# A gated linear attention feeding a silu layer on one core: silu tiles kept in matmul order, stores in two transfers, and a new order of the instructions

## The chip, the cores and the metric

The kernel runs on one core of one Trainium2 chip. The core has a matrix engine (TensorE, PE in the profile; its weight loads are PEld), a vector engine (VectorE, DVE), a scalar engine for table functions (ScalarE, ACT), GpSimd (POOL) and SyncE (SP), which here only issues transfers. All of them share sixteen DMA engines. The metric is the device time of one execution in microseconds: 178.47 us median of three runs before the change (178.16 to 179.44).

## The reference

For each of 4 batches and 8 heads, a 48 x 48 state is decayed row by row and updated at each of 768 steps, and read with q. The results of all heads form rows of 384 numbers, which go through a layer of 2048 units with silu:

```python
f = 1.0 / (1.0 + np.exp(-f_logit))
for t in range(S):                                   # 768 steps
    state = f[:, :, t, :, None] * state + np.einsum('bhd,bhe->bhde', k[:, :, t], v[:, :, t])
    y[:, :, t] = np.einsum('bhd,bhde->bhe', q[:, :, t], state)
x = y.transpose(0, 2, 1, 3).reshape(3072, 384)       # tokens by (head, dim)
h = x @ w_in                                         # 384 -> 2048
out = (h / (1.0 + np.exp(-h))) @ w_out               # 2048 -> 384
```

Inputs and the output are float32; the matmuls take bfloat16.

## The kernel before, in words

The 768 steps are cut into three windows of 256 tokens. A window of one batch is a block, numbered 4 x window + batch, so there are twelve blocks (0 to 11), and block D + 4 needs the state that block D leaves. A partition holds two neighbouring tokens (r = 0 and 1), so a block of 256 tokens fills 128 partitions, and inside a block there are two chunks of 64 partitions (f = 0 and 1).

The program is a list of tokens, the string PLAN, and `emit` turns each token into its instructions. The order of the tokens is the order in which each engine gets its instructions; nothing is reordered later. A token is a kind, a block and mostly a half of the heads, and `@v`, `@p`, `@a` or `@s` names the engine where there is a choice (VectorE, GpSimd, ScalarE, SyncE). Every tile lives in one of a fixed number of buffers per class (the table SLOTS), handed out in the order of the list, so the order also sets which transfer or matmul waits for which buffer. There are 8 PSUM banks, 21 wide buffers for loads and 4 output buffers.

The kinds that the text speaks of:

- ldf, ldq, ldk, ldv (L278): loads of a block's gate, q, k and v, of 384 KB each, or halves of 192 KB for blocks 0 and 1. WI and WO (L413, L415) load the layer's weights, CI and CO cast them to bfloat16.
- E, L, F1, IA, A, AX (L280 to L298): exponentials and logarithms of the gates on ScalarE; SA and CS sum them (CS on PE, L288 and L291). They and silu need different function tables, so ScalarE loads a table at each turn (L426).
- K1, KI, Q1, QG (L302 to L313): q and k times their decays.
- TQ with QC, or TD (L326): the transpose of q and k, on PE for the first blocks and by a DMA transpose for blocks 4 to 11. SC (L335) are the score matmuls, two PSUM banks a token; AT (L341) masks them; Y, YS (L349, L356) form the outputs.
- DP, SD, SU (L374 to L381): the state's increment, sum and decay.
- YC, then YT with XC or YD (L368): the output's copy out of PSUM and its transpose, into the tile xT.
- MI (L390): six matmuls, xT by 256 columns of w_in: one hidden group. SI (L394): silu of that group into the tile hT. MO (L400): four matmuls of hT by w_out: one output group; four of them make 128 tokens' outputs. OC copies them out of PSUM, SO (L408) stores a block.
- W (L422): matmuls on an idle tile, which fill PE's time where it would otherwise wait.

The outputs' partitions have two tokens' places interleaved until silu: the token at (f, r, c) is row 128 f + 2 c + r of its block. Before the change silu itself puts the tokens in their order while it writes hT, so that an output tile's partitions are consecutive rows. One line does that, with steps of two elements on the written side:

```python
nc.scalar.activation(T[1][:, 2 * j:2 * j + 2].rearrange("p n (f c r) -> p (n f) r c", f=2, r=2),
                     T[0].rearrange("p (m r c) -> p m r c", m=4, r=2), AF.Silu)
```

The last block's second half of tokens (f = 1) is computed in two column ranges (LAST: 0 to 256, 256 to 384) that are copied and stored apart, and its first half by itself.

Of the kernel before, what the change touches and what calls it, by code (L numbers as in the profile page):

```python
# [24 lines left out]
    ldf.1.1@s E.1.1 L.1.1 SA.1.1@v W.19:CS.1.1 CS.1.1 W.2:CS.0.0 ldf.0.0@s E.0.0 L.0.0 SA.0.0@v CS.0.0 W.4:CS.0.1  # L25
    ldf.0.1@s ldq.1.1@s ldk.1.1@s ldq.0.0@s ldf.1.0@s E.0.1 IA.1.1 L.0.1 F1.0.0 A.1.1 AX.0.0 F1.1.1 F1.0.1 IA.0.0
    Q1.1.1@v K1.1.1@v SA.0.1@p CS.0.1 W.8:TQ.1.1 A.0.0 IA.0.1 A.0.1 E.1.0 KI.1.1@p QG.1.1@v ldq.0.1@s ldk.0.1@s L.1.0
    TQ.1.1 W.8:CS.1.0 QC.1.1@a K1.0.1@p ldk.0.0@s ldq.1.0@s ldk.1.0@s ldv.0.1@s ldf.2@s ldv.0.0@s ldv.1.1@s ldv.1.0@s
    Q1.0.0@v SA.1.0@p CS.1.0 IA.1.0 F1.1.0 AX.1.0 A.1.0 QG.0.0@v Q1.0.1@v QG.0.1@v KI.0.1@v K1.0.0@p KI.0.0@p SC.1.1
    TQ.0.1 W.3:TQ.0.0 AX.0.1 QC.0.1@a K1.1.0@p KI.1.0@p AM.0@p Q1.1.0@v TQ.0.0 W.2:SC.0.1 AT.1.1 QG.1.0@v ldf.3@s  # L30
    WI.0@s WI.5@s WI.4@s ldq.2@s WI.2@s ldk.2@s WI.1@s WI.3@s WI.7@s WI.6@s ldv.2@s WO.0@s WO.1@s SC.0.1 W.5:TQ.1.0
    AT.0.1 TQ.1.0 QC.0.0@a E.2.0 AX.1.1 L.2.0 SC.0.0 W.3:DP.0 AT.0.0 VB.0@p SA.2.0@p DP.0 VB.1@p QC.1.0@a E.2.1
    CS.2.0 L.2.1 AX.2.0 SA.2.1@p AM.1@p SU.0.0@v SC.1.0 Y.0.0 Y.0.1 YC.0.0@a F1.2.0 IA.2.0 E.3.1 DP.1 AT.1.0 YS.0.1
    W.3:Y.1.0 CI.0@p SU.1.0@v YC.0.1@v Y.1.0 Y.1.1 YS.1.1 F1.2.1 E.3.0 YC.1.1@a CI.5@p YC.1.0@v YT.0.0 YT.0.1 CS.2.1
    XC.0.1@a XC.0.0@v YT.1.1 YT.1.0 AX.2.1 L.3.0 L.3.1 SA.3.1@p CI.2@p MI.0.0 XC.1.1@v XC.1.0@v CI.7@p F1.3.0 CI.4@a
    A.2.0 MI.1.0 IA.2.1 A.2.1 VB.2@p AM.2@p SD.1.1 SD.0.1 Q1.2.0@v Q1.2.1@v SA.3.0@v QG.2.1@v QG.2.0@v K1.2.0@v
    KI.2.0@v WO.2@s ldf.4@s WO.3@s ldq.3@s ldk.3@s WO.4@s WO.7@s WO.5@s ldk.4@s WO.6@s ldq.4@s MI.1.5 MI.1.4 MI.0.4
    MI.0.5 SI.1.4 MI.0.2 SI.0.5 SI.1.5 CS.3.0 CS.3.1 MI.1.2 SI.0.2 SI.1.0 SI.0.0 TQ.2.0 CI.1@v MI.1.1 MI.0.1 SI.1.2
    SI.0.4 SI.1.1 SI.0.1 K1.2.1@v KI.2.1@v CI.3@v TQ.2.1 QC.2.0@v QC.2.1@v CO.0@p CO.1@p MI.0.3 SI.0.3 SC.2.0 SC.2.1
    AT.2.0 AT.2.1 CI.6@a MI.0.7 MI.1.7 MI.1.6 MI.1.3 SI.1.7 SI.0.7 SI.1.6 SI.1.3 DP.2 Y.2.0 Y.2.1 ldf.6@s ldv.4@s  # L40
    ldv.3@s MI.0.6 SU.2.0@v YS.2.1 SI.0.6 E.4.0 IA.3.0 F1.3.1 L.4.0 IA.3.1 E.4.1 A.3.0 L.4.1 AX.3.0 F1.4.0 AX.3.1
    A.3.1 F1.4.1 CO.2@p K1.3.0@p SA.4.0@p KI.3.0@p SU.0.1@p K1.3.1@p SA.4.1@p KI.3.1@p K1.4.1@p CO.6@p K1.4.0@p
    YC.2.0@v YT.2.0 XC.2.0@v YC.2.1@v SD.2.1 MO.1.1.0 MO.0.1.0 YT.2.1 XC.2.1@v CO.3@v MO.0.0.0 MO.1.0.0 MI.2.7 MI.2.3
    MO.1.0.1 MO.0.0.1 MO.0.1.1 MO.1.1.1 Q1.3.0@v Q1.3.1@v QG.3.0@v QG.3.1@v MI.2.2 SI.2.7 SI.2.2 MI.2.1 SI.2.1 SI.2.3
    MI.2.0 MI.2.6 SI.2.6 SI.2.0 MI.2.4 MI.2.5 SI.2.4 CO.4@v CO.7@v SU.2.1@v CO.5@v TQ.3.0 MO.2.1.0 MO.0.0.2 SI.2.5
    QC.3.0@a MO.1.1.2 CS.4.1 MO.2.1.1 CS.4.0 MO.0.1.2 IA.4.1 MO.0.1.3 TQ.3.1 AX.4.1 IA.4.0 MO.2.1.2 MO.2.1.3 A.4.1
# [55 lines left out]
LAST = ((0, 256), (256, 384))  # L102

SET_OF = {x: "natural_log_exp_and_others" for x in ("E", "L", "F1", "IA", "A", "AX")} | {"SI": "silu_and_others"}


def uses(t):

# [18 lines left out]
    if kind == "CS":  # L127
        return [I("s", D), I("ps", "cs", D, a[1])]
# [359 lines left out]
```

## Time and profile before

| what | value |
|---|---|
| median of 3 runs | 178.47 us (178.16 to 179.44) |
| the profiled execution's own time | 179.7 us |
| its span in the profile | 178.0 us |
| PE busy | 169.2 us, 95% |
| PE's weight loads | 127.6 us, 72% |
| ACT busy | 134.8 us, 76% |
| DVE busy | 102.3 us, 57% |
| POOL busy | 62.2 us, 35% |
| DMA | 36.02 MB, mean 202 GB/s |
| granted clock of PE | full in all slices |

A row of a group reads: line, engine, operation, tile written <- tile read, shape, count; then busy time in us, mean ns of one; then the engine's idle time just before them and what ended it. A row of a timeline has its start and length in us, then engine, line, operation and count, and in brackets the idle time before it with what ended it. A matmul's end is modelled, so a busy PE is not necessarily PE at its peak, and back-to-back instructions overlap, so a group's busy time is less than count times mean.

### The profile page before, as it was taken

The page shows a single profiled execution, that of the slowest core. Times are in us where ns is not written, and L with a number is a line of the kernel's source. Part 1 is how long each engine was busy: PE and PEld are TensorE (multiplying, and loading weights), DVE is VectorE, ACT ScalarE, POOL GpSimd, SP SyncE. Part 2 cuts the span into 40 slices and gives each one's busy share as a digit, 9 for nine tenths or more (in the row PEclk, how much of TensorE's full clock was granted, in tenths as well). Part 3 has the DMA queues.
Part 4 walks back from the last instruction along what each step waited for, and adds up shares of the span by engine and source line. Part 5 has one row for each costly group of instructions (what it writes and reads, how often), then busy time and mean ns, then how long its engine had stood idle before and what let it go on. Part 6 is the DMA issues. An engine that isn't in the chain of part 4 may idle for free.

```text
span 178.0 us, 5593 instructions
## 1 busy us (share of the span) xinstructions
PE 169.2 (95%) x2281; PEld 127.6 (72%) x2281; DVE 102.3 (57%) x247; ACT 134.8 (76%) x289; POOL 62.2 (35%) x106
## 2 busy tenths in 40 slices
PE   7789999999999999999999999999979999999992
PEld 5567787867767787767688767688747688866661
DVE  6499887569148992497755586597784520000021
ACT  4989999799999899779899976899624029892410
POOL 6389512639562595104642230464003000000010
PEclk9999999999999999999999999999999999999999
DMA  5999999999929999999999998786993526000033
GB/s 136 296 299 323 311 344 363 333 292 341 258 40 215 299 130 230 201 267 269 155 206 247 213 297 225 174 209 120 315 208 103 90 48 251 18 0 0 0 131 137
DMA packets 81850, 36.02 MB, mean 202 GB/s; under 512 B 73824, under 2 KB 81664, under 8 KB 81824
## 3 DMA queue, kind: packets, MB, share of 16 engines
q1 hardware_dynamic: 81184, 34.35, 77.5%
q0 software_dynamic: 224, 0.79, 1.1%
q10 hardware_dynamic: 416, 0.52, 0.8%
q8 instruction: 18, 0.29, 0.7%
q14 instruction: 8, 0.07, 0.1%
HBM read 25.17 MB, written 4.72 MB: 168 GB/s over the span
## 4 chain that ended last, share of the span: by engine, by line
PE 46%; issue 20%; ACT 12%; DMA 10%; SPq 8%; DVE 1%; POOL 1%; DVEq 0%; ACTq 0%; POOLq 0%
PE ps L400 23%; PE ps L390 14%; ACT hT L394 11%; SPq L278 7%; DMA wide<-in_moe_w_in_dram 4%; DMA qkT<-qk 3%; DMA out_dram<-o 3%; PE ps L335 2%; PE ps L349 2%; SPq L413 2%; PE ps L356 2%; PE ps L288 1%; PE ps L374 1%; DVE sd L379 1%; PE ps L322 1%
## 5 line engine op out<-in xcount | busy, mean ns | idle before, releaser
L394 ACT ACTIVATE hT<-ps 128x512 bf16<-128x512 f32 x96 | 60.2, 788 | 13.7 <-PE ps L390 13.5
L400 PE MATMUL ps<-w_out_sb,hT 128*128 128x384 bf16 (+2 forms) x400 | 67.9, 320 | 0.2 <-ACT hT L394 0.2
L390 PE MATMUL ps<-xT,w_in_sb 128*128 128x256 bf16 x576 | 66.4, 273 | 0.4 <-DMA xT<-yb 0.3
L390 PEld LDWEIGHTS <-w_in_sb 128*128 128x128 bf16 x576 | 55.5, 98 | 9.1 <-DMA xT<-yb 0.6
L400 PEld LDWEIGHTS <-hT 128*128 128x128 bf16 x400 | 36.7, 98 | 21.0 <-ACT hT L394 0.2
L341 DVE TENSOR_TENSOR atm<-ps,mask 128x512 bf16<-128x512 f32 x48 | 30.3, 682 | 5.8 <-PE ps L335 5.5
L274 DVE COPY o<-ps 128x384 f32<-128x384 f32 (+2 forms) x9 | 4.6, 508 | 31.5 <-issue 28.2
L313 DVE TENSOR_TENSOR qk<-wide,ps 128x192 bf16<-128x192 f32 x48 | 14.4, 346 | 7.9 <-ACT ps L296 5.6
L308 POOL TENSOR_TENSOR qk<-wide,ia 128x192 bf16<-128x192 f32 x24 | 15.0, 647 | 5.3 <-ACT ar L298 2.9
L274 ACT COPY o<-ps 128x384 f32<-128x384 f32 x16 | 7.6, 482 | 11.4 <-PE ps L400 10.0
L286 POOL TENSOR_TENSOR s<-lf 128x192 bf16<-128x192 bf16 x15 | 8.5, 570 | 21.5 <-ACT lf L282 16.9
L381 POOL TENSOR_TENSOR st<-sd,al 128x384 bf16<-128x384 f32 x12 | 10.2, 855 | 15.1 <-DVE sd L379 7.6
L302 POOL TENSOR_TENSOR wide<-wide,f 128x192 f32<-128x192 f32 x17 | 11.0, 654 | 10.1 <-DMA wide<-in_k_dram 9.7
L379 DVE TENSOR_TENSOR sd<-ps,st 128x384 f32<-128x384 f32 x16 | 8.6, 550 | 9.1 <-PE ps L374 7.0
L280 ACT ACTIVATE e<-wide 128x384 f32<-128x384 f32 x24 | 12.0, 519 | 1.6 <-DMA wide<-in_f_logit_dram 1.4
L408 POOL DMA_DIRECT2D out_dram<-o x2 | 1.6, 816 | 32.4 <-ACT o L274 32.4
L282 ACT ACTIVATE lf<-e 128x384 bf16<-128x384 f32 x24 | 11.9, 520 | 0.3
L308 DVE TENSOR_TENSOR qk<-wide,ia 128x192 bf16<-128x192 f32 x24 | 10.5, 482 | 2.1 <-POOL wide L302 2.0
L426 ACT ACT_TABLE_LOAD x9 | 11.5, 1283 | 0.2
L274 POOL CAST vb<-wide 128x768 bf16<-128x768 f32 x7 | 5.8, 832 | 14.8 <-DMA wide<-in_v_dram 14.4
L422 PE MATMUL ps<-idle 128*128 128x256 bf16 x57 | 9.8, 320 | 1.3 <-DVE idle L434 1.3
L304 DVE SCALAR_TENSOR_TENSOR wide<-e,wide 128x192 f32<-128x192 f32 x24 | 9.9, 434 | 1.6 <-DMA wide<-in_q_dram 1.6
(60 smaller groups left out, 170.2 us busy)
## 6 DMA issues: line engine op xcount, KB each, us to landing
wide<-in_f_logit_dram SPq DMA_DIRECT2D x10, 384.0 KB, 5.5
wide<-in_q_dram SPq DMA_DIRECT2D x10, 384.0 KB, 6.2
wide<-in_k_dram SPq DMA_DIRECT2D x10, 384.0 KB, 5.8
wide<-in_v_dram SPq DMA_DIRECT2D x10, 384.0 KB, 5.5
wide<-in_moe_w_in_dram SPq DMA_DIRECT2D x8, 384.0 KB, 6.2
wide<-in_moe_w_out_dram SPq DMA_DIRECT2D x8, 384.0 KB, 6.3
out_dram<-o SPq DMA_DIRECT2D x8, 384.0 KB, 3.9
wide<-in_f_logit_dram SPq DMA_DIRECT2D x4, 192.0 KB, 3.2
```

The source lines that it names most:

```text
L274: copy = lambda o, i: E.copy(o, i) if eng == "a" else E.tensor_copy(o, i)
L278: E.dma_start(out=T[0][:, hs], in_=SRC[kind[2]][w, b][:, hs])
L280: nc.scalar.activation(T[1][:, hs], T[0][:, hs], AF.Exp, scale=-1.0)
L282: nc.scalar.activation(T[1][:, hs], T[0][:, hs], AF.Ln, bias=1.0)
L302: E.tensor_mul(T[1][:, hs, 0:d], T[1][:, hs, 0:d], T[0][:, hs])
L308: E.tensor_mul(T[2][:, g, 1, :, r, :, 0:d], T[0][:, hs, r * d:r * d + d].rearrange("p (n x) d -> p n x d", x=2), T[1][:, hs].rearrange("p ...
L313: E.tensor_mul(T[2][:, g, 0, :, r, :, 0:d], T[0][:, hs, r * d:r * d + d].rearrange("p (n x) d -> p n x d", x=2), T[1][:, 0:4 * d].rearrang ...
L341: nc.vector.tensor_mul(T[2][:, g, x], T[x].rearrange("p (s n c) -> p s n c", s=2, n=2), mask.rearrange("p s r c -> p s (r c)")[:, :, None, ...
L390: nc.tensor.matmul(h[:, i, 128 * fs.start:128 * fs.stop], w_in_sb[:, j, kk, i * 128:i * 128 + 128], T[0][:, fs, kk], start=(kk == 0), stop ...
L394: nc.scalar.activation(T[1][:, 2 * j:2 * j + 2].rearrange("p n (f c r) -> p (n f) r c", f=2, r=2), T[0].rearrange("p (m r c) -> p m r c", ...
L400: nc.tensor.matmul(T[1][:, 0:cols.stop - cols.start], T[0][:, n, f * 128:f * 128 + 128], w_out_sb[:, n, cols], start=(n == 0), stop=(n == ...
L426: nc.scalar.preload_act_table_set(turn[name])
```

## The change

Three things change together.

First, the list PLAN is a new one, found by a search; it has the same tokens but for some fills W (65 matmuls in place of 57), some changes of engine after the @, and another order. The diff below shows one of its lines, where the hidden groups of blocks 3 and 4 end and the scores of 5 and 6 begin.

Second, silu writes hT in the order that it reads, except for block 11. The output tile of blocks 0 to 10 then has partition 64 r + c for the token 2 c + r, so its store goes in two transfers, one for each r, of 64 partitions each, with every second row of the output as target. Block 11 keeps the old order, and its three pieces are stored as before.

Third, the stores are issued by other engines: blocks 1, 2, 3, 4, 6, 8, 9 and 10 by GpSimd, 5 by ScalarE, 0 and 7 by SyncE; block 11's pieces by ScalarE, SyncE and ScalarE, in that order. Before, SyncE had eight whole blocks, ScalarE one (8), GpSimd two (4 and 10).

The code for an empty tuple SINGLE takes no part: no block is in it. The two columns that AX reads move from column 192 to column 384 of their PSUM bank.

```diff
 PLAN = """
-    MI.4.3 MI.4.0 SI.4.3 SI.4.0 MI.4.2 SI.4.2 DP.6 DP.5 SC.6.0 SC.5.0 TD.6.1 TD.5.1 SD.6.0 AT.6.0 AT.5.0 SD.5.0
+    SI.4.0 SI.4.4 SI.4.6 DP.5 DP.6 SC.6.0 MO.4.1.0 MI.4.7 MO.4.1.1 MO.4.1.2 SI.4.7 SD.5.0 SD.6.0 SU.5.0@p SU.6.0@p
...
-    dst = out.rearrange("(b w f t) n -> b w t f n", b=B, f=2, t=128)
+    dst = out.rearrange("(b w f p r) n -> b w r p f n", b=B, f=2, p=64, r=2)
...
-                nc.tensor.matmul(T[1][:, 4 * d + 2 * n:4 * d + 2 * n + 2], T[0][:, 4 * g + 2 * n:4 * g + 2 * n + 2, :],
-                                 tri[:, 63::64], start=False, stop=True, skip_group_check=True)
+                    nc.tensor.matmul(T[1][:, 8 * d + 2 * n:8 * d + 2 * n + 2], T[0][:, 4 * g + 2 * n:4 * g + 2 * n + 2, :],
+                                     tri[:, 63::64], start=False, stop=True, skip_group_check=True)
...
         elif kind == "SI":
             j = a[1]
-            nc.scalar.activation(T[1][:, 2 * j:2 * j + 2].rearrange("p n (f c r) -> p (n f) r c", f=2, r=2),
-                                 T[0].rearrange("p (m r c) -> p m r c", m=4, r=2), AF.Silu)
+            if D == BLOCKS - 1:
+                nc.scalar.activation(T[1][:, 2 * j:2 * j + 2].rearrange("p n (f c r) -> p (n f) r c", f=2, r=2),
+                                     T[0].rearrange("p (m r c) -> p m r c", m=4, r=2), AF.Silu)
+            else:
+                nc.scalar.activation(T[1][:, 2 * j:2 * j + 2], T[0].rearrange("p (n c) -> p n c", n=2), AF.Silu)
...
         elif kind == "SO":
-            fs = slice(0, 2) if g is None else slice(g, g + 1)
-            cols = slice(*LAST[a[2]]) if len(a) == 3 else slice(0, d_model)
-            E.dma_start(out=dst[b, w][:, fs, cols], in_=T[0][:, fs, cols])
+            if g is None:
+                for r in range(2):
+                    E.dma_start(out=dst[b, w, r], in_=T[0][64 * r:64 * r + 64])
+            else:
+                cols = slice(*LAST[a[2]]) if len(a) == 3 else slice(0, d_model)
+                E.dma_start(out=out[(b * WINDOWS + w) * 256 + 128 * g:(b * WINDOWS + w) * 256 + 128 * g + 128, cols], in_=T[0][:, g, cols])
```

Three places show how the instructions move. The first is SyncE's queue while blocks 9, 11 and 10 get their q and k transposed. Before, qk_100 belongs to block 11, qk_98 to 9 and qk_101 to 10; wide_76 and wide_61 take k of blocks 9 and 10, wide_77 and wide_62 v of 9 and 11; two output transposes (xT) stand just ahead of these rows:

```order
L278 DMA wide_76<-in_k_dram 128x8x96
L278 DMA wide_77<-in_v_dram 128x8x96
L278 DMA wide_61<-in_k_dram 128x8x96
L326 DMA_TRANSPOSE qkT_107<-qk_100 128x8x128
L326 DMA_TRANSPOSE qkT_106<-qk_98 128x8x128
L278 DMA wide_62<-in_v_dram 128x8x96
L326 DMA_TRANSPOSE qkT_107<-qk_100 128x8x128
L408 DMA out_dram<-o_124 128x2x384
L326 DMA_TRANSPOSE qkT_106<-qk_98 128x8x128
L326 DMA_TRANSPOSE qkT_105<-qk_101 128x8x128
```

Now, with qk_99 for block 11, qk_100 for 9, wide_62 and wide_61 for k of 9 and 10, and the output transposes of blocks 8 and 7 in the rows:

```order
L383 DMA_TRANSPOSE xT_116<-yb_112 128x6x128
L282 DMA wide_62<-in_k_dram 128x8x96
L383 DMA_TRANSPOSE xT_114<-yb_111 128x6x128
L282 DMA wide_61<-in_k_dram 128x8x96
L341 DMA_TRANSPOSE qkT_107<-qk_99 128x8x128 x2
L341 DMA_TRANSPOSE qkT_106<-qk_100 128x8x128
L282 DMA wide_80<-in_v_dram 128x8x96
L341 DMA_TRANSPOSE qkT_106<-qk_100 128x8x128
L282 DMA wide_81<-in_v_dram 128x8x96
L282 DMA wide_78<-in_v_dram 128x8x96
```

Block 9's k moved ahead of block 7's output transpose, the v loads behind the transposes, block 11's two transposes ahead of block 9's, and the store out of the rows.

The second place is the end of the engines that finish the output. On VectorE before, the last six instructions, with o the output buffers:

```order
L274 CAST yb_112<-ps_129 128x384
L274 CAST yb_112<-ps_132 128x384
L274 COPY o_125<-ps_134 128x384
L274 COPY o_123<-ps_128 128x384
L274 COPY o_124<-ps_129 128x256
L274 COPY o_126<-ps_132 128x128
```

On ScalarE now, its last six, among them two stores of block 11's pieces:

```order
L278 COPY o_124<-ps_129 128x384
L278 COPY o_126<-ps_130 128x384
L278 COPY o_126<-ps_128 128x384
L429 DMA out_dram<-o_125 128x384
L278 COPY o_124<-ps_132 128x128
L429 DMA out_dram<-o_124 128x128
```

The last copy moved from VectorE to ScalarE, and from the buffer that block 10 used (o_126 before) to the one that block 9 used (o_124 now; block 10's is o_126 in both).

The third place is on PE where block 6's first scores end. Before, with qkT_106 of block 6 and qkT_107 of block 5:

```order
L335 MATMUL ps_132<-qkT_106 64x128
L335 LDWEIGHTS qkT_106
L335 MATMUL ps_127<-qkT_106 64x128
L335 LDWEIGHTS qkT_107
L335 MATMUL ps_131<-qkT_107 64x128
```

Now, with qkT_107 of block 6:

```order
L350 MATMUL ps_131<-qkT_107 64x128
L350 LDWEIGHTS qkT_107
L350 MATMUL ps_127<-qkT_107 64x128
L418 LDWEIGHTS hT_118
L418 MATMUL ps_129<-w_out_sb,hT_118 128x384
```

Block 5's first scores followed at once before; an output group of block 4 follows now, and three more groups stand ahead of block 5's scores.

More of the change, by code (lines that the diff above doesn't have):

```diff
@@ L30 @@
[L30 to L34, printed above, removed]
@@ L93 @@
+    MO.11.1.3.0 MO.11.1.0.1 OC.11.1.0@v SO.11.1.0@s MO.11.1.1.1 MO.11.1.2.1 MO.11.1.3.1 OC.11.1.1@a SO.11.1.1@a
 """
@@ L127, in uses @@
     if kind == "CS":
+        return [I("lf" if D in SINGLE else "s", D), I("ps", "cs", D, a[1])]
+    if kind == "CT":
         return [I("s", D), I("ps", "cs", D, a[1])]
     if kind == "IA":
-        return [I("ps", "cs", D, a[1]), I("ia", D)]
+        return [I("ps", "cs", D, a[1]), I("wide", "ia", D) if D in SINGLE else I("ia", D)]
     if kind == "A":
@@ L141, in uses @@
     if kind == "KI":
-        return [I("wide", "k", D), I("ia", D), I("qk", D)]
+        return [I("wide", "k", D), I("wide", "ia", D) if D in SINGLE else I("ia", D), I("qk", D)]
     if kind == "QG":
```

170 lines of the change are left out of this document (93 added, 77 removed).

## The prediction

> **What bounds the kernel now.** I read the page's busy shares first, then TensorE's windows, then its timeline for each gap in it.
>
> ```profile
> span 178.0 us, 5593 instructions
> PE 169.2 (95%) x2281; PEld 127.6 (72%) x2281; DVE 102.3 (57%) x247; ACT 134.8 (76%) x289; POOL 62.2 (35%) x106
> ```
>
> TensorE is busy 95% of the span. The windows (first number behind the stretch: its length; then busy time of PE, PEld, DVE, ACT, POOL; last three: granted clock, DMA share, GB/s) show where the other 5% lie:
>
> ```profile
> 0.00:10.00 10.00, 7.54 (x56) 5.61 (x57) 6.11 (x31) 7.67 (x20) 5.12 (x17) 1.00 0.86 225
> 10.00:20.00 10.00, 9.44 (x238) 7.12 (x236) 9.56 (x20) 9.20 (x23) 8.09 (x15) 1.00 1.05 306
> ...
> 20.00:170.00 150.00, 147.74 (x1953) 111.70 (x1951) 84.84 (x194) 117.91 (x248) 48.36 (x75) 1.00 0.80 197
> ...
> 170.00:178.00 8.00, 4.45 (x41) 3.15 (x39) 1.83 (x4) 0.00 (x0) 0.62 (x1) 1.00 0.43 150
> ...
> L422 PE MATMUL ps<-idle 128*128 128x256 bf16 x57 | 9.8, 320 | 1.3 <-DVE idle L434 1.3
> ```
>
> The first 20 us hold 2.46 + 0.56 = 3.02 us of idle PE and 9.8 us of fill matmuls (tokens W) that stand where PE would wait. The last 8 us hold 3.55 us. In the 150 us between them PE is idle for 2.26 us in all, at full clock. The change adds and removes no useful matmul, so in that stretch a new order cannot win more than these 2.26 us. They lie here (PE's timeline; in brackets the idle time before the piece and who ended it):
>
> ```profile
> 29.60 0.41 PE L335 MATMUL ps<-qkT 48*64 48x128 bf16 x15 [0.20 <-ACT hT L394]
> 30.19 0.42 PE L335 MATMUL ps<-qkT 48*64 48x128 bf16 x16 [0.17 <-ACT hT L394]
> ...
> 68.08 4.76 PE L390 MATMUL ps<-xT,w_in_sb 128*128 128x256 bf16 x42 [0.34 <-DMA xT<-yb]
> ...
> 74.38 0.41 PE L335 MATMUL ps<-qkT 48*64 48x128 bf16 x15 [0.36 <-ACT hT L394]
> ...
> 100.81 2.11 PE L400 MATMUL ps<-w_out_sb,hT 128*128 128x384 bf16 x12 [0.16 <-ACT hT L394]
> ...
> 131.28 0.42 PE L335 MATMUL ps<-qkT 48*64 48x128 bf16 x16 [0.93 <-DMA qkT<-qk]
> 165.15 9.30 PE L400 MATMUL ps<-w_out_sb,hT 128*128 128x384 bf16 x72
> ```
>
> Four waits for silu (0.20 + 0.17 + 0.36 + 0.16 = 0.89 us, either the PSUM bank that silu frees or its tile), two for a DMA transpose (0.34, 0.93). They sum to 2.16 of the 2.26.
>
> **Silu in matmul order.** It concerns 88 of 96 instructions (all but block 11's eight).
>
> ```profile
> L394 ACT ACTIVATE hT<-ps 128x512 bf16<-128x512 f32 x96 | 60.2, 788 | 13.7 <-PE ps L390 13.5
> L280 ACT ACTIVATE e<-wide 128x384 f32<-128x384 f32 x24 | 12.0, 519 | 1.6 <-DMA wide<-in_f_logit_dram 1.4 <-DVE wide L304 0.2
> L274 ACT COPY qkT<-ps 128x1024 bf16<-128x1024 bf16 x6 | 6.1, 1010 | 0.1
> L274 ACT COPY o<-ps 128x384 f32<-128x384 f32 x16 | 7.6, 482 | 11.4 <-PE ps L400 10.0 <-issue 1.3
> ...
> 65.26 9.06 ACT L394 ACTIVATE hT<-ps 128x512 bf16<-128x512 f32 x15
> ```
>
> No row has a silu written contiguously. The two copies give (1010 - 482) / 640 = 0.825 ns an element, so from the contiguous 384-element exponential I estimate 519 + 128 x 0.825 = 625 ns against 788. Back to back, the 15 take (9.06 - 0.79) / 14 = 591 ns each; with about 0.1 us of overlap, 525 would do. Bounds: 788 and 591 as now, 625 and 525; I take the lower pair, since every contiguous form of ACT lies on one line. This frees up to 88 x 0.066 = 5.8 us of ScalarE, but ScalarE is not the bound: in the row at 68.08 PE makes 42 hidden matmuls, seven groups of six, in 4.76 us, 0.66 us a group after the tail of the last; a silu of 591 ns already keeps up with that, and only the backlog from the table load before it is worked off sooner. What reaches the end is the 0.89 us of waits. The pair at 30 us is fed by a ScalarE that also casts weights there, so I credit half of 0.37; the one at 74.38 goes, also because the new order puts four other matmul groups (some 2.6 us) between the two score groups that asked for four PSUM banks at once; the one at 100.81 goes. Gain 0.18 + 0.36 + 0.16 = 0.70, between 0 and 0.89.
>
> The Trainium skill, page "SBUF — State Buffer", section "Door 1: The DMA port swizzle", has a rule that speaks against this: an engine may step up to 8 bf16 elements for free, as long as two accesses fall into each 16-byte line. The old step was 2 elements, so by it 788 would stay; the trace's straight line says otherwise, and what the rule would do is the first rival.
>
> **The new order.** Of the joints between blocks, one had a dear wait: at 131.28 the transposes of blocks 9 to 11.
>
> ```profile
> 116.06 1.25 POOL L302 TENSOR_TENSOR wide<-wide,f 128x192 f32<-128x192 f32 x2 [2.32 <-DMA wide<-in_k_dram]
> ...
> 110.90 1.22 SPq L368 DMA_TRANSPOSE xT<-yb  x1
> ...
> 119.91 1.37 POOL L308 TENSOR_TENSOR qk<-wide,ia 128x192 bf16<-128x192 f32 x2
> ...
> 114.74 8.93 PE L390 MATMUL ps<-xT,w_in_sb 128*128 128x256 bf16 x78
> ...
> 125.58 1.71 SPq L326 DMA_TRANSPOSE qkT<-qk  x1
> ...
> qkT<-qk SPq DMA_TRANSPOSE x16, 3.4
> xT<-yb SPq DMA_TRANSPOSE x8, 2.9
> ```
>
> K of block 9 came at 116.06, GpSimd waited for it, and the last transpose that PE then waited for left at 125.58. Its load stood behind two output transposes (the second at 110.90); now it stands between them, one transpose of 1.22 us earlier: K at 114.8. GpSimd makes 9's K products next (1.25 for the two), then 11's second product (1.37 for such a pair in the row at 119.91): 117.4. From there 11's second transpose and 9's two leave 1.3 us apart, with one V load of 0.6 between: 117.4, 118.7, 120.6; 3.4 after that they are there: 120.8, 122.1, 124.0. PE starts its run of hidden groups at 114.74 less the 0.52 won by then, and asks for the first pair of scores (11 and 9) after 15 groups of 0.66, at 124.1, for the other pair three or four us later. So 0.93 goes, with 2 us to spare. Bounds: 0 to 0.93.
> The wait at 68.08 has the same queue ahead of it (five loads, then the transpose), so it stays: 0, between -0.34 and +0.5. The other joints stand at the same count of matmuls as before. The tightest is block 9's first hidden group: its output copy (0.48) and transpose (2.9) must be done while PE makes five output groups (3.3) and some small ones (about 1.5), so about 1 us is left after the queue ahead of the copy on ScalarE; block 7's second score group keeps as little. For a new wait I charge 0.2, bounds 0 and 1.3.
> The first 18 DMAs are the same loads in another order, and the first weight tile is the 19th in both; the first hidden group starts after the same attention work but one transpose. I take 0, bounds ±0.7 (one half-size load). The 65 fills instead of 57 stand where PE waits for these loads; without that cover they would cost 8 x 0.1 us.
>
> **Stores.** All eleven whole-block stores become two transfers of 64 partitions: sixteen issues on GpSimd, two on ScalarE, four on SyncE. ScalarE's two (0.35 each by its store row below) stand among the exponentials ahead of the hidden groups of 7 and 8, where PE has eight PSUM banks to run ahead in.
>
> ```profile
> L408 POOL DMA_DIRECT2D out_dram<-o x2 | 1.6, 816 | 32.4 <-ACT o L274 32.4
> ...
> out_dram<-o SPq DMA_DIRECT2D x8, 384.0 KB, 3.9
> out_dram<-o POOLq DMA_DIRECT2D x2, 384.0 KB, 5.0
> ```
>
> GpSimd pays 14 more issues x 0.816 = 11.4 us, but is busy 48 of the middle 150 us. Queued behind are state updates: store 2 ahead of block 8's (1.6 us, which leaves it about 0.8 before PE asks), store 6 ahead of 11's and 10's (asked for over 4 us later). Cost 0; without that cover 1.6 each.
>
> **The tail.**
>
> ```profile
> 169.88 4.89 DMA out_dram<-o
> ...
> 172.10 3.55 SPq L408 DMA_DIRECT2D out_dram<-o  x3
> 174.11 0.35 ACTq L408 DMA_DIRECT2D out_dram<-o  x1
> ...
> 174.99 0.29 DVE o L274
> ...
> out_dram<-o SPq DMA_DIRECT2D x1, 64.0 KB, 1.5
> ```
>
> PE ends at 165.15 + 9.30 = 174.45. Those 72 matmuls are ten whole output groups and pieces worth four more, 0.66 us a group. The last copy waits until 174.99 for block 10's store, whose buffer it takes. Now it takes block 9's buffer: after 9's last group PE still has eleven groups' worth, 7.3 us; less the copy, the store leaves 6.6 us ahead of PE's end, its second half 0.8 later, and even a landing of 4.89 comes in time. The copy starts about 0.45 us sooner. Against it, block 10's last group ends six groups' worth, 4.0 us, ahead of PE's end; less the copy and the first half's issue its second half leaves 2.6 ahead and with 4.89 lands 2.3 behind PE's end. Today's last store leaves at 175.3 and lands in 1.5, 2.4 behind. So gain 0.45 if the second half lands faster than that, 0 if not; I take 0.45, since 4.89 was a whole store.
>
> **Sum.** 0.70 + 0.93 + 0.45 - 0.2 = 1.88 us. The profiled execution took 179.7 us with a span of 178.0, so it goes to 177.8; the median of the runs, 178.47, to 176.6.
>
> **Rivals.** *Layout free.* Silu stays at 788 ns: then only the order counts, and 74.38 and 100.81 keep their waits. 0.93 + 0.45 - 0.2 = 1.2: 177.3. For it: silu is the only table function of its kind in these rows; against it the line of the others.
>
> *Slower: transposes beside stores.* Stores on GpSimd's own queue no longer wait their turn behind SyncE's transposes.
>
> ```profile
> 64.00:66.00 2.00, 2.00 (x21) 1.80 (x19) 2.00 (x9) 1.99 (x3) 2.00 (x5) 1.00 1.95 97
> ...
> 70.00:72.00 2.00, 2.00 (x21) 1.79 (x19) 0.46 (x1) 2.00 (x5) 0.00 (x0) 1.00 1.25 270
> ```
>
> At 70 transposes run alone at 270 GB/s; at 64 one is mixed with loads and the queues, though counted as full, move 97: about 2 x (1 - 97/270) = 1.3 us lost. Stores 3 and 2 now leave near block 7's transposes, 1 and 6 near 10's, 4 near the output transposes. A collision decides once the joint's slack (0.8 to 1 us) is gone. Two that reach PE give 178.47 - 1.88 + 2.6 = 179.2, three 180.5. Against it: old stores stood between transposes, too, and PE waited once.
> The same page of the Trainium skill, section "SBUF: two separate sides", warns that VectorE's fast modes keep GpSimd from writing descriptors, so that its DMAs start late; the two issues here took 748 and 884 ns, the longer one beside a busy VectorE, so no run shows more than that yet.
>
> *Better start.* If the new start also wins its 0.7 and the wait at 68.08 goes, 178.47 - 1.88 - 0.7 - 0.34 - 0.2 = 175.4; down to 174.4 if stretched matmuls shrink too.
>
> **Chances.** Forecast 0.60, layout free 0.12, slower rival 0.18, better start 0.10. A measurement of this kernel cannot tell under 1% (1.8 us) from no change. Within the forecast (175.6 to 177.9 by the bounds) somewhat over half lies under 176.7: 0.36 faster, 0.24 the same. Layout free: 0.01 and 0.11. Slower rival: two collisions count as the same (0.04), three as slower (0.14). Better start: faster. Together 0.47, 0.39, 0.14. The range goes from 174.9 to 179.4, which leaves out three collisions and the best starts.
>
> **What would show it.** Right: silu near 625 ns; no wait of PE over 0.3 us around the scores of 9 and 11; the last copy within 0.15 us of PE's end. Wrong: silu at 788; PE waiting on qkT or xT for more than 1 us at any joint; PE's first hidden matmul later than 21 us; GpSimd issues well over 0.9 us.

## The result and the profile after

Over twenty executions of each kernel the changed one took 177.68 us (176.08 to 179.32), the one before 179.28 us (178.16 to 180.97): a ratio of 0.990, 95% interval 0.987 to 0.993. Measured again beside the first experiments it was 0.991 (0.987 to 0.995). So the change wins about 1.7 us. The forecast was 1.9 us: 176.6 against the 178.47 of the first three runs, which lay 0.8 us under the median of twenty. A ratio here leaves out executions more than 1.5% above the fastest of the same kernel: three of the changed kernel's twenty, and in the experiments, for instance, five of the twelve of the kernel whose silu steps where it reads (180.4 to 181.4 us).

The profiled execution took 176.33 us. The page's first lines and its chain of waits:

```profile
span 174.6 us, 5617 instructions
PE 168.4 (96%) x2289; PEld 128.6 (74%) x2289; DVE 101.7 (58%) x248; ACT 123.4 (71%) x287; POOL 72.1 (41%) x121
...
PE 83%; SPq 9%; DMA 4%; DVE 1%; issue 1%; ACT 0%; ACTq 0%
```

The chain now runs through TensorE for 83% of the span, 46% before. The windows (columns as before) show why:

```profile
0.00:10.00 10.00, 7.57 (x58) 5.74 (x58) 5.27 (x27) 7.47 (x22) 6.29 (x19) 1.00 0.83 216
10.00:20.00 10.00, 9.76 (x241) 7.78 (x240) 9.96 (x24) 9.40 (x20) 7.03 (x13) 1.00 1.05 301
...
20.00:170.00 150.00, 149.93 (x1983) 114.07 (x1982) 86.00 (x199) 106.23 (x246) 58.83 (x90) 1.00 0.83 202
170.00:174.60 4.60, 1.18 (x19) 0.98 (x17) 0.42 (x1) 0.27 (x1) 0.00 (x0) 1.00 0.47 133
```

From 20 to 170 us PE idles 0.07 us, where it idled 2.26. All six waits that the prediction listed are gone. The groups behind the terms:

```profile
L413 ACT ACTIVATE hT<-ps 128x512 bf16<-128x512 f32 x88 | 45.8, 626 | 14.7 <-PE ps L405 14.3
...
L410 ACT ACTIVATE hT<-ps 128x512 bf16<-128x512 f32 x8 | 5.8, 762 | 1.5 <-PE ps L405 1.5
...
L426 POOL DMA_DIRECT2D out_dram<-o x16 | 9.9, 619 | 29.7 <-ACT o L278 26.3
```

Silu in matmul order takes 626 ns; block 11's eight in the old form take 762. A half store costs GpSimd 619 ns. SyncE's queue where blocks 11 and 9 are prepared (start, length, instruction):

```profile
112.41 5.64 SPq L341 DMA_TRANSPOSE qkT<-qk  x3
118.11 0.57 SPq L282 DMA_DIRECT2D wide<-in_v_dram  x1
118.77 2.10 SPq L341 DMA_TRANSPOSE qkT<-qk  x1
```

PE's timeline at the same place, with the first hidden group of blocks 7 and 8 and the two pairs of scores:

```profile
112.94 3.33 PE L405 MATMUL ps<-xT,w_in_sb 128*128 128x256 bf16 x29
...
122.85 0.64 PE L350 MATMUL ps<-qkT 48*64 48x128 bf16 x32
...
126.78 0.64 PE L350 MATMUL ps<-qkT 48*64 48x128 bf16 x32
```

The end, in the timeline of all engines:

```profile
167.72 3.45 PE L418 MATMUL ps<-w_out_sb,hT 128*128 128x384 bf16 x36
168.05 1.18 POOL L426 DMA_DIRECT2D out_dram<-o  x2 [2.07 <-ACT o L278]
...
171.26 0.27 ACT L278 COPY o<-ps 128x128 f32<-128x128 f32 x1 [3.50 <-PE ps L418]
171.55 0.34 ACTq L429 DMA_DIRECT2D out_dram<-o  x1
```

Block 11's first transpose leaves at 112.41; the first one of this group left at 117.59 before. Both pairs of scores start without a wait. The last copy starts 0.1 us behind PE's end; before it was 0.54.

**A common point in both orders.** PE's first hidden group of blocks 7 and 8 (at 114.74 before, 112.94 after) is a good place to cut the span: in both orders the same 680 matmuls lie behind it. PE's timeline gives, for the kernels below (the experiments follow; starts and ends are of one execution, ratios of medians):

| kernel | that group starts | PE ends | between | ratio of the times |
|---|---|---|---|---|
| before | 114.74 | 174.45 | 59.71 | 1 |
| before, second profile | 114.79 | 173.90 | 59.11 | 1.001 |
| changed | 112.94 | 171.18 | 58.24 | 0.990 |
| changed, second profile | 113.90 | 172.14 | 58.24 | 0.991 |
| layout only, old order | 112.50 | 174.94 | 62.44 | 1.000 |
| new order, silu as before | 116.68 | 175.70 | 59.02 | 0.997 |
| layout and one mended joint, old order | 113.66 | 173.78 | 60.12 | 0.996 |

58.24 us in both profiles of the changed kernel is PE's floor for this stretch (it also came out in each profile of the kernels with the new order and a short silu further down). The first pair of profiles differs by 3.27 us at PE's end, the second pair by 1.76, which is what the medians say: the first profile of the changed kernel was one of its shortest executions. Two rows are of long ones: "layout only" of 180.31 us (its median is 179.29), "new order, silu as before" of 180.34 us (178.84).

### The profile page after: what moved, and what is told of

Its sections match the earlier page's. It is cut to its first block, busy times and chain, and to the rows that moved or that the text cites. A ratio compares the mean times of both kernels' runs of the same rounds, so it can differ in the third digit from the quotient of the medians.

```text
span 174.6 us, 5617 instructions
## 1 busy us (share of the span) xinstructions
PE 168.4 (96%) x2289; PEld 128.6 (74%) x2289; DVE 101.7 (58%) x248; ACT 123.4 (71%) x287; POOL 72.1 (41%) x121
## 4 chain that ended last, share of the span: by engine, by line
PE 83%; SPq 9%; DMA 4%; DVE 1%; issue 1%; ACT 0%; ACTq 0%
PE ps L418 36%; PE ps L405 33%; SPq L282 7%; DMA wide<-in_k_dram 4%; PE ps L350 3%; PE ps L364 3%; PE ps L371 2%; SPq L434 2%; PE ps L389 2%; PE ps L337 1%; PE ps L298 1%; DVE qk L328 1%; PE ps L379 0%; PE ps L302 0%; DVE wide L317 0%
## 5 line engine op out<-in xcount | busy, mean ns | idle before, releaser
L405 PE MATMUL ps<-xT,w_in_sb 128*128 128x256 bf16 x576 | 67.1, 273 | 0.0
L413 ACT ACTIVATE hT<-ps 128x512 bf16<-128x512 f32 x88 | 45.8, 626 | 14.7 <-PE ps L405 14.3
L278 DVE COPY o<-ps 128x384 f32<-128x384 f32 (+1 forms) x11 | 5.9, 541 | 32.2 <-PE ps L418 32.2
L426 POOL DMA_DIRECT2D out_dram<-o x16 | 9.9, 619 | 29.7 <-ACT o L278 26.3
L278 ACT COPY o<-ps 128x384 f32<-128x384 f32 (+1 forms) x14 | 6.4, 465 | 16.2 <-PE ps L418 16.2
L396 POOL TENSOR_TENSOR st<-sd,al 128x384 bf16<-128x384 f32 x13 | 10.9, 845 | 11.9 <-DVE sd L394 11.9
L328 POOL TENSOR_TENSOR qk<-wide,ia 128x192 bf16<-128x192 f32 x22 | 13.2, 621 | 5.4 <-DVE wide L317 4.7
L317 POOL TENSOR_TENSOR wide<-wide,f 128x192 f32<-128x192 f32 x14 | 9.0, 639 | 13.2 <-DMA wide<-in_k_dram 12.2
L328 DVE TENSOR_TENSOR qk<-wide,ia 128x192 bf16<-128x192 f32 x26 | 12.5, 527 | 1.8 <-POOL wide L317 1.7
L443 PE MATMUL ps<-idle 128*128 128x256 bf16 x65 | 10.3, 318 | 1.3 <-DVE idle L455 1.3
```

The costliest lines, as they stand in the source:

```text
L278: copy = lambda o, i: E.copy(o, i) if eng == "a" else E.tensor_copy(o, i)
L328: E.tensor_mul(T[2][:, g, int(kind == "KI"), :, r, :, 0:d], T[0][:, hs, r * d:r * d + d].rearrange("p (n x) d -> p n x d", x=2), decay.rea ...
L396: E.tensor_mul(T[2].rearrange("p n (x d) -> p n x d", d=d), T[0][:, 0:HD].rearrange("p (n x d) -> p n x d", n=4, d=d) if "ps" in mine[0] e ...
L405: nc.tensor.matmul(h[:, i, 128 * fs.start:128 * fs.stop], w_in_sb[:, j, kk, i * 128:i * 128 + 128], T[0][:, fs, kk], start=(kk == 0), stop ...
L413: nc.scalar.activation(T[1][:, 2 * j:2 * j + 2], T[0].rearrange("p (n c) -> p n c", n=2), AF.Silu)
L443: nc.tensor.matmul(T[0][:, 0:256], idle[:, 0:128], idle[:, 0:256], start=True, stop=True, skip_group_check=True)
```

## Experiments

**The changed kernel again**, unaltered.

> The changed kernel once more, unaltered, beside the others. The first measurement gave a ratio of 0.990 to the kernel before (1.8 us), but the two profiled executions lay 3.4 us apart, and single executions of one kernel spread over 3 us. All theories: ratio 0.987 to 0.993. If its profiled execution is a slower one (span near 176), its stretch from 20 to 170 us shows where one execution of the same program loses more than another: either idle PE (over 0.3 us, at waits for DMA) or the same busy time with stretched matmuls.

Ratio 0.991. Its profile (span 175.6 us) has two waits in PE's timeline that the first had not:

```profile
29.55 2.79 PE L405 MATMUL ps<-xT,w_in_sb 128*128 128x256 bf16 x24 [0.17 <-DVE w_in_sb L278]
...
108.16 1.46 PE L418 MATMUL ps<-w_out_sb,hT 128*128 128x384 bf16 x8 [0.29 <-DVE yb L278]
```

It is 0.96 us later than the first profile by the common point, and equal from there on. So what differs from one execution to the next lies in the first 114 us here, not behind them.

**Layout only**: the changed code with the old list.

```diff
 PLAN = """
-    (the new list)
+    (the list of the kernel before, each store on its old engine)
```

> Silu contiguous and stores in two parts, but the order and the engines of the kernel before. Theory (silu's layout and the order each win their own waits, and add): the waits for silu go (0.70 of 0.89 us), the wait on qkT of 0.93 and the late last copy stay, so 0.4 to 0.8 us are won: ratio 0.995 to 0.998. Rival, the layout does it all: ratio 0.990. Rival, the order does it all: ratio 1.000, with silu at 625 ns all the same.

Ratio 1.000 (0.997 to 1.004): nothing. Yet silu takes 617 ns, and PE is at the common point 2.2 us sooner. First two windows of the kernel before, then the same two of this one and four later ones (the second number is PE's busy time, the third from the end the granted clock):

```profile
20.00:60.00 40.00, 39.52 (x522) 29.71 (x520) 27.23 (x62) 38.23 (x77) 19.87 (x31) 1.00 0.95 279
60.00:100.00 40.00, 39.30 (x549) 31.00 (x547) 25.80 (x62) 35.60 (x82) 17.01 (x27) 1.00 1.06 215
```

```profile
20.00:60.00 40.00, 39.99 (x529) 30.36 (x529) 28.20 (x65) 36.55 (x80) 20.58 (x32) 1.00 0.98 284
60.00:100.00 40.00, 40.00 (x568) 31.70 (x567) 26.29 (x64) 34.53 (x82) 17.12 (x28) 1.00 1.05 218
...
128.00:130.00 2.00, 0.23 (x16) 0.07 (x7) 1.56 (x4) 0.00 (x0) 0.00 (x0) 1.00 0.72 144
130.00:132.00 2.00, 1.91 (x22) 1.06 (x23) 1.29 (x2) 0.00 (x0) 0.00 (x0) 0.69 0.93 213
132.00:134.00 2.00, 2.00 (x8) 0.95 (x7) 0.00 (x0) 0.00 (x0) 0.82 (x1) 0.50 1.20 293
134.00:136.00 2.00, 2.00 (x67) 1.49 (x67) 0.56 (x1) 0.96 (x2) 0.00 (x1) 0.95 0.21 76
```

PE's timeline of this kernel at the common point and at the scores of block 9:

```profile
112.50 3.77 PE L405 MATMUL ps<-xT,w_in_sb 128*128 128x256 bf16 x31
...
130.09 0.42 PE L350 MATMUL ps<-qkT 48*64 48x128 bf16 x16 [1.86 <-DMA qkT<-qk]
```

All waits for silu are gone, and the gain is more than those waits show: from the first hidden group to the common point the four profiles with the old order and the old silu need 94.3 to 94.4 us each, this one 91.95. Of the 2.4 us PE's idle time was 1.3 (0.48 + 0.70 in the two windows, 0.16 behind them; 0.01 now). Both programs give PE the same matmuls in the same order, so the trace tells, from each matmul's start to the next one's, where the whole lies. All but 0.1 to 0.2 us of it is at five places (us; "shown" is the idle time in brackets, "lost" what the step takes longer than in the layout-only kernel):

| PE waits for | first profile, shown | lost | second profile, shown | lost |
|---|---|---|---|---|
| silu, near 30 us | 0.37 | 0.70 | 0.17 | 0.42 |
| silu, near 74 us | 0.36 | 0.57 | 0.56 | 1.04 |
| silu, near 101 us | 0.16 | 0.23 | 0.16 | 0.23 |
| a cast of w_in, near 25 us | 0.10 | 0.26 | 0.45 | 0.62 |
| block 4's output transpose, near 68 us | 0.34 | 0.50 | 0 | 0 |

So a wait costs more than its brackets show. They count from the modelled end of the matmul before. The hidden groups' matmuls before the change:

```profile
L390 PE MATMUL ps<-xT,w_in_sb 128*128 128x256 bf16 x576 | 66.4, 273 | 0.4 <-DMA xT<-yb 0.3
```

One has a mean of 273 ns, but 576 of them take 66.4 us, 115 ns each; the difference, 0.16 us, is what the last two rows lose beyond what they show. Silu's waits, 0.89 us by the brackets in both profiles, cost 1.5 and 1.7 us (1.5 and 1.8 in the two mended joints with the old silu further down). The last two rows are not silu's and change from one execution to the next: the two mended joints with the short silu need 93.2 and 92.8 us to the common point, with waits of 1.05 and 0.54 us for casts. So the layout is worth some 1.5 to 1.8 us up to there, and the rest of the 2.4 was this execution's luck.

Then PE comes 2 us early to the scores of 9 and 11. Three of their four transposes come earlier too (1.2 to 2.1 us); block 9's second doesn't. SyncE's queue just ahead of it, first in the kernel before, then in this one:

```profile
122.17 2.68 SPq L326 DMA_TRANSPOSE qkT<-qk  x1
124.95 0.53 SPq L408 DMA_DIRECT2D out_dram<-o  x1
125.58 1.71 SPq L326 DMA_TRANSPOSE qkT<-qk  x1
```

```profile
120.03 3.69 SPq L341 DMA_TRANSPOSE qkT<-qk  x1
123.81 1.28 SPq L426 DMA_DIRECT2D out_dram<-o  x2
125.20 3.61 SPq L341 DMA_TRANSPOSE qkT<-qk  x2
```

It leaves at 125.20 (before 125.58, in the second profile 124.90), behind a transpose that takes 3.69 us to issue and behind store 6, now two issues, and PE waits 1.86 us for it. Behind that wait the granted clock falls (0.69, 0.50, then 0.95): (0.31 + 0.50 + 0.05) x 2 = 1.7 us more. Together 3.6 us, and the gain is gone in this execution. Of the kernel's twelve executions only this one and one other have a mean clock of 0.99; the others take 177.8 to 180.6 us, and no profile shows where they lose. The number is the one of the rival "the order does it all", but not its reason: the layout does win, and in the profiled execution loses it at the next joint. The theory and the rival "the layout does it all" both missed that.

**Order only**: the new list with its engines; silu in steps of two and whole stores, as before.

```diff
-            if D == BLOCKS - 1:
-                (block 11's silu, steps of two) ... else: (contiguous)
+            (steps of two for all blocks; every store whole)
```

> The new order and engines, but silu written in steps of two elements for all blocks and whole stores, as before. Theory: the wait on qkT, the one on xT and the late copy go, but with silu at 780 to 790 ns waits for it come back, 0.4 to 0.8 us of them in the stretch from 20 to 170 us: ratio 0.993 to 0.996. Rival, the layout does it all: 1.000. Rival, the order does it all: 0.990, and PE does not wait for silu.

Ratio 0.997 (0.994 to 1.001), a little above the theory's 0.993 to 0.996 and far from the 0.990 of "the order does it all". Silu takes 800 ns, and four waits for it are back, of 0.17 us each in brackets. From start to start, against the changed kernel, these four places lose 1.4 us, which is about what separates 0.997 from 0.990 (1.3 us): in the new order the layout's gain comes through. This profile also has one wait of 1.83 us for a transpose of blocks 7 and 8 (it left at 96.6 and landed at 104.6), which no other profile of this order shows. Layout 0.000, order -0.003, both -0.010, each known to 0.003 or 0.004: they don't seem to add; the layout pays under the new order and not under the old.

**One joint of the old order mended.** Three attempts, all in the list. The first moves block 9's k load ahead of block 7's output transpose, block 11's second transpose ahead of 9's, a v load and store 6 behind them:

```diff
-YD.7 MI.7.1 ... ldk.9@s ... KI.9.0@v ... TD.11.1 ... KI.11.0@v QG.11.0@v ... TD.9.0 ldv.11@s TD.11.0 SO.6@s TD.9.1
+ldk.9@s YD.7 MI.7.1 ... KI.11.0@v QG.11.0@v KI.9.0@v ... TD.11.1 TD.11.0 ... TD.9.0 TD.9.1 ldv.11@s SO.6@s
```

> The kernel before with one joint put as in the new order: on SyncE's queue block 9's k load ahead of block 7's output transpose, block 11's second transpose ahead of block 9's two, one v load and store 6 behind them; VectorE makes 11's products ahead of one of 9's. Silu and stores as before. Theory (the 0.93 us term by itself): PE no longer waits on qkT near 131 us, nothing else is late next, and the time falls by 0.6 to 0.9 us: ratio 0.995 to 0.997. Rival (something else at that joint is late next, or the waits of one execution are not those of the others): the wait goes but the ratio is 0.998 to 1.002.

Ratio 1.011 (1.007 to 1.015): slower. The wait didn't go, it moved and doubled (PE's timeline):

```profile
128.72 0.64 PE L335 MATMUL ps<-qkT 48*64 48x128 bf16 x32 [1.98 <-DMA qkT<-qk]
```

VectorE made 9's product only after both of 11's, so 9's transpose left at 123.64 and not at 120.22 (1.3 us of it is a late start of this execution, told in the last section), and block 9's scores were still the first to be asked. The second attempt asks 11's scores first and lets VectorE make 11's products earlier, with both layouts of silu (its main lines):

```diff
-Q1.11.1@v QG.11.1@v Q1.10.0@v ... QG.10.0@v KI.11.1@v ... QG.10.1@v ... Q1.11.0@v QG.9.1@v
+Q1.11.1@v QG.11.1@v KI.11.1@v Q1.11.0@v QG.11.0@v KI.11.0@v Q1.10.0@v ... QG.10.0@v ... QG.10.1@v ... QG.9.1@v
-SC.9.0 SC.11.1 ... SC.11.0 SC.9.1
+SC.11.0 SC.11.1 ... SC.9.0 SC.9.1
```

> Silu contiguous and stores in two parts in the old order (as in the layout-only kernel, ratio 1.000), and one joint mended: k of blocks 9 and 10 loaded around block 7's output transpose, VectorE makes both of block 11's q and k products ahead of those of 10 and 9, block 11's two transposes leave first, its scores are asked first, one v load and store 6 stand behind the transposes. Theory (what silu wins ahead of 124 us is given back at this joint, where PE then waits longer for qkT): with the joint mended the wait of 1.86 us shrinks below 0.5 and the two together win 0.8 to 1.7 us: ratio 0.991 to 0.996. Rival (the joint is only one of many places where the new order helps): ratio 0.997 to 1.001.

> The same joint mended, but silu in steps of two elements and whole stores as in the kernel before. Theory: without silu's gain PE comes later to the joint, so less waits there: PE's wait on qkT near 131 us goes and 0.4 to 0.9 us are won: ratio 0.995 to 0.998. Rival (another wait follows at once, as in the first attempt at this joint): ratio 1.000 or above, and the trace names the wait.

With the short silu 0.996 (0.993 to 0.998), with the old one 1.009 (1.005 to 1.013). The two have one list and differ in silu and the store halves; their medians, measured side by side, are 2.2 us apart, so with the joint mended this way the layout pays under the old order, too. In both the wait for qkT is gone, and another stands in its place. One row of PE's timeline of each, the short silu first:

```profile
118.71 5.40 PE L405 MATMUL ps<-xT,w_in_sb 128*128 128x256 bf16 x48 [1.41 <-DVE qk L328]
```

```profile
120.28 5.40 PE L390 MATMUL ps<-xT,w_in_sb 128*128 128x256 bf16 x48 [1.42 <-DVE qk L313]
```

A hidden group waits for a PSUM bank that block 10's gates still fill, since VectorE reads them behind 11's products. The third attempt takes that away (short silu):

```diff
-QG.11.1@v KI.11.1@v Q1.11.0@v QG.11.0@v KI.11.0@v Q1.10.0@v ... QG.10.1@v
+QG.11.1@v KI.11.1@p Q1.11.0@v QG.11.0@v Q1.10.0@v ... QG.10.1@v KI.11.0@v
```

> The mended joint with contiguous silu in the old order, whose trace showed 1.41 us of PE waiting near 118 us for a PSUM bank that VectorE still had to read (block 10's QG behind three products of block 11). Here one of those products is GpSimd's and the other stands behind block 10's two QG. Theory (layout and joint together are most of the gain, once no new wait takes their place): the bank wait shrinks below 0.5 us, no wait on qkT over 0.3, and the ratio goes from 0.9956 to 0.988 to 0.992. Rival (the new order helps at many places that are not this joint): ratio stays at 0.994 or above although both waits are gone.

Ratio 1.010 (1.005 to 1.015), far from the theory's. It is above the rival's 0.994, but not for the rival's reason. In PE's timeline the bank wait shrinks, and a third one appears:

```profile
119.28 4.10 PE L405 MATMUL ps<-xT,w_in_sb 128*128 128x256 bf16 x36 [0.50 <-DVE qk L328]
...
126.53 0.51 PE L389 MATMUL ps<-vb,qk 64*128 64x96 bf16 x8 [1.85 <-DVE vb L278]
```

Block 9's v load left at 120.00, behind a transpose of 118.72 and beside the two halves of store 4 (119.09 and 119.86), and landed at 125.89; in the second attempt it left at 119.04 and landed at 123.38. In nine of this kernel's twelve executions the mean granted clock was 0.979 to 0.991, and they took 182.5 us in the median; the other three 179.7, 0.7 above the kernel before. So most of the 1.010 is the clock.

So the mended joint alone never paid, and only one of the two attempts with the short silu may have given a part (0.996 against the 1.000 of the layout alone, with intervals that overlap). The new list differs at this joint in more than my three edits: GpSimd makes 11's first k product at 98.07 (VectorE at 109.30 before) and VectorE the second at 105.37, q and k work is shared out differently, and 9's v load stands between its two transposes.

**Stores by SyncE** instead of GpSimd, halves as in the changed kernel:

```diff
-SO.1@p ... SO.2@p ... SO.3@p ... SO.4@p ... SO.6@p ... SO.8@p ... SO.9@p ... SO.10@p
+SO.1@s ... SO.2@s ... SO.3@s ... SO.4@s ... SO.6@s ... SO.8@s ... SO.9@s ... SO.10@s
```

> The changed kernel with the eight stores of GpSimd issued by SyncE instead, at the same places of the list, still two parts each. Theory (the stores' engine costs nothing, it only has to have room): 0.990 to 0.992 as the changed kernel, unless a store on SyncE's queue waits for its output copy and holds up the q, k, v loads or transposes behind it; the places of stores 3, 2, 1 and 6 stand among such transfers, so 0 to 1 us is lost: ratio 0.990 to 0.996. Rival (stores on GpSimd's queue collide with transposes and cost 1.3 us each): moving them away wins, ratio below 0.988.

Ratio 0.989 (0.985 to 0.994): no difference from the changed kernel. From 20 to 170 us PE idles 0.53 us, nearly all of it at one weight cast (0.50 at 25.34).

**Silu steps where it reads.** The new list; silu of all twelve blocks writes hT contiguously in token order and reads PSUM in steps of two, so every store is whole again:

```diff
-nc.scalar.activation(T[1][:, 2 * j:2 * j + 2], T[0].rearrange("p (n c) -> p n c", n=2), AF.Silu)
+nc.scalar.activation(T[1][:, 2 * j:2 * j + 2].rearrange("p n (f c r) -> p (n f) c r", f=2, r=2),
+                     T[0].rearrange("p (m r c) -> p m c r", m=4, r=2), AF.Silu)
```

> The changed kernel's order, but silu of all blocks writes hT contiguously in token order and takes the step of two on the side that it reads, four-byte elements of PSUM; so the stores go whole. It tells what the old layout's cost was. If the stepped two-byte write was it: silu near 626 ns and ratio 0.990 (or a little below, with half the stores). If stepping on either side costs: silu near 790 ns or above and the ratio of the order-only kernel, 0.997.

> The kernel with silu stepping on the read side and whole stores once more, since its 0.985 came from four executions. If it is better than the changed kernel: 0.984 to 0.988. If it is the changed kernel by another road: 0.989 to 0.992.

The group of silu in the first of this kernel's two profiles:

```profile
L409 ACT ACTIVATE hT<-ps 128x512 bf16<-128x512 f32 x96 | 49.8, 618 | 17.3 <-PE ps L405 17.0
```

618 ns with the step on the read side, against 762 to 800 with it on the written side. Ratios 0.985 (0.981 to 0.989) and 0.987 (0.982 to 0.992), from four and three executions; over all twelve the median is 177.5 us, that of the changed kernel 177.7. So it is no worse than the changed kernel, without its second store half and its other partition order; that it is better isn't shown.

One difference shows at the end. Under the new order the last store leaves 0.38 us behind PE's end in every profile, but with store halves (changed kernel twice, stores by SyncE) the span ends 3.4 to 3.5 us behind PE's end, with whole stores (order only, this kernel twice, the next one) 2.9 to 3.2. Block 10's second half lands 0.6 to 1.1 us behind PE's end, its whole store at least 0.25 ahead of it, and the last piece 2.1 to 2.4 behind with halves, 1.9 to 2.1 with whole stores. So the halves cost 0.2 to 0.5 us there.

> The same with its eight GpSimd stores issued by SyncE, whole blocks. If the engine of the stores makes no difference, as with halves (0.989 against 0.991): the ratio of the kernel with GpSimd's whole stores, within 0.004. If a collision of GpSimd's stores with transposes costs anything, it is faster by that.

With its stores on SyncE as well: 0.984 (0.980 to 0.988), 176.54 us in the median, the best kernel here and 2.4 us below the kernel before in its own comparison. Against the changed kernel's 0.990 and 0.991 the intervals still overlap a little, so its lead over it is likely, not shown.

**The kernel before again**, unaltered.

> The kernel before, unaltered, as a kernel of its own: ratio 1.000 within 0.004. Its second profile shows how much of the 3.4 us between the first two profiled executions belongs to one execution: the wait on qkT near 131 us between 0.3 and 2 us, the four waits for silu unchanged within 0.1 us each, and in the stretch from 20 to 170 us more useful matmul work than in the first profile if stretched matmuls are a matter of the single execution.

Ratio 1.001 (0.997 to 1.004). Its profile (span 177.4 us) idles 1.78 us from 20 to 170, and it has the silu waits (0.17, 0.18, 0.38, 0.16), but no wait for qkT near 131 us, where 0.3 to 2 us were expected, and none for xT near 68; in their place are 0.45 us for a weight cast at 24.93 and 0.32 for v at 134.74. PE's timeline at two of the silu waits, then at the scores of 11 and 9:

```profile
73.84 0.21 PE L335 MATMUL ps<-qkT 48*64 48x128 bf16 x1 [0.18 <-ACT hT L394]
74.43 0.41 PE L335 MATMUL ps<-qkT 48*64 48x128 bf16 x15 [0.38 <-ACT hT L394]
...
125.15 0.64 PE L335 MATMUL ps<-qkT 48*64 48x128 bf16 x32
...
129.74 0.93 PE L335 MATMUL ps<-qkT 48*64 48x128 bf16 x32
```

## Why the prediction was right, and where only its sum was

The time came out as forecast, 1.7 us for 1.9, and silu's length, the missing waits at the scores and the early last copy came as foretold. But three terms of the sum were mis-sized, silu's too small, the order's and the tail's too large, and that these errors cancel is luck.

- **"A new order cannot win more than these 2.26 us."** Wrong as a bound. The first pair of profiles shows 3.27 us at PE's end, and the layout alone cut 2.4 us ahead of the common point, where the idle rows held 1.3. The brackets count from a matmul's modelled end and show less than a wait costs (0.34 for 0.50 at the output transpose).
- **Silu, 625 ns and 0.70 us.** The duration was right (626, and the line of the contiguous forms held); the gain was mis-sized. The step was: the waits count as their brackets show them, 0.89 us at most. They cost 1.5 to 1.8 us in the old order, and 1.4 is won back in the new one. The rival "layout free" is out by 626 against 762, and so is what the Trainium skill's page "SBUF — State Buffer", section "Door 1: The DMA port swizzle", would give for a step of two bf16 elements (no cost): on ScalarE's writes it costs 140 to 180 ns of 620 here.
- **The order, 0.93 us for the wait at 131.28.** This was one execution's wait. The second profile of the kernel before has none there, and with the short silu in the old order it was 1.86. My path for it was wrong too: I let block 11's second transpose leave at 117.4 and 9's at 118.7 and 120.6, on k of block 9; 11's left at 112.41 and 115.39 and 9's at 116.78 and 118.77, because 11's products are made earlier. What the order is worth shows behind the common point: 58.24 us, PE's floor, against 59.1 to 59.7 before and 62.4 with the layout alone. It takes in the 0.9 to 1.8 us that PE arrives earlier. That the terms add was the failed assumption: alone they gave 0.0 and 0.5 us (each uncertain by 0.7), together 1.7.
- **The wait at 68.08 "stays".** It went: block 4's output transpose left at 62.50 and had landed by 65.2, where before it landed at 68.0. But the second profile of the kernel before has no wait there either (it landed at 67.4), so this, too, was one execution's. For new waits I charged 0.2 us; the first profile shows none, the second 0.46 (0.17 + 0.29).
- **Start 0.** Right: the first hidden group at 20.48 and 20.39, before at 20.41 and 20.39.
- **Stores at no cost.** Right for the engine: moving them off GpSimd changes nothing measurable, and a half store's issue took 619 ns, not the 816 of a whole one. Not for the halves, which cost 0.2 to 0.5 us at the end. The slower rival (transposes beside stores) shows nowhere in the changed kernel's two profiles. In the order-only profile the transpose that landed after 7.9 us has a whole store of GpSimd beside it (97.05 to 104.60), and four loads; in the changed kernel, beside two halves, it took 4.9. Whether the store did it isn't shown.
- **Tail, 0.45 us.** The copy starts 0.37 to 0.47 us sooner, as worked out, and block 10's second half left 2.5 us ahead of PE's end, 2.6 by the forecast, landing 1.1 behind it. But the last store then needed 1.72 us to land, not 1.54, and the span ends 3.4 and 3.5 us behind PE's end, before 3.5 and 3.5: at most 0.1 us won. The term left out what follows the copy, and the halves slow that.

What stays open: how the 1.7 us splits between the many differences of the new list, its eight more fills among them. The layout-only profile shows the joint of blocks 9 to 11 taking the layout's gain away, and the pair with the mended joint (2.2 us apart) agrees; which entries of the new list keep the gain isn't shown.

## What to carry to other kernels

When the engine that bounds the kernel is sped up in one stretch, follow it to the next joint where it meets something that doesn't move with it: here the layout alone put PE 2 us ahead, and the profiled execution lost more than that 15 us later to a DMA transpose and the clock behind the wait. Where two programs give an engine the same instructions in the same order, compare start with start: idle time in brackets showed 0.89 us of waits that cost 1.5 to 1.8. Before a wait in one profile becomes a term, look whether a second execution has it; the waits for silu came to 0.89 us in both profiles, a wait for a DMA went from 0.93 to none. And where a write has to step, try the step on the side that is read.

## What the hardware showed that I had not expected

- **Twice PE's clock halved for 3.4 us right behind a wait of 1.8 us.** Besides the one in the layout-only kernel, the first attempt at the joint has it near the start. PE's timeline there:

```profile
8.44 0.24 PE L288 MATMUL ps<-s,tri 128*128 128x192 bf16 x1 [1.83 <-POOL s L286]
```

  The windows of this kernel there:

```profile
8.00:10.00 2.00, 1.56 (x12) 1.21 (x12) 1.27 (x5) 2.00 (x10) 1.35 (x3) 0.74 0.99 250
10.00:12.00 2.00, 2.00 (x15) 1.68 (x14) 1.87 (x6) 1.67 (x3) 1.95 (x4) 0.50 1.09 266
12.00:14.00 2.00, 2.00 (x39) 1.73 (x37) 2.00 (x4) 1.26 (x7) 1.92 (x4) 0.91 1.08 297
```

  The loss is (0.26 + 0.50 + 0.09) x 2 = 1.7 us, or 3.4 us at half clock, as in the other case; the trace's clock records have 3.41 us in both, from 0.5 and 0.7 us after the wait's end. Waits of 1.83 and 1.85 us in two other profiles, and one of 1.98 later in this one, had no such drop, so that the wait sets it off is argued from the order in time, and something else decides, too. The Trainium skill, page "TensorE: Matmul & The Clock Gate", section "HAM oscillation — how this bites in real kernels", sets the limit at gaps over about 3.4 us; the length of the drop agrees with that window, the gap ahead of it was here 1.8 us. So such a wait may cost 3.5 us and not 1.8.
- **ScalarE's step costs on one side only**: 762 to 800 ns for a bf16 write in steps of two, 618 for the float32 read of PSUM in steps of two, 614 to 628 for neither. Side, memory and element size change together here; which of them matters isn't shown.
- **A DMA transpose or a load among others varies by microseconds**: over all profiles transposes of q and k landed between 3.0 and 7.9 us after they left, v loads between 3.6 and 8.9.
